# Loading w_in and the first v's through SyncE's queue in 4 bytes, with the rounding on ScalarE

## The chip, the cores and the metric

The kernel runs on one core of a Trainium2 chip. The metric is the device time of one execution in microseconds (us). The core has TensorE (PE; its weight loads are listed as PEld), VectorE (DVE), ScalarE (ACT), GpSimd (POOL) and SyncE (SP). Transfers are issued by SyncE's queue, by ScalarE's queue or by GpSimd, and are carried by 16 DMA engines.

## The reference

The work has two stages. The first is a gated linear attention over 4 batches, 8 heads, 768 positions and 48 channels, in float32:

```python
f = 1.0 / (1.0 + np.exp(-f_logit))
for t in range(S):
    state = f[:, :, t, :, None] * state + np.einsum('bhd,bhe->bhde', k[:, :, t], v[:, :, t])
    y[:, :, t] = np.einsum('bhd,bhde->bhe', q[:, :, t], state)
```

The second takes y as 3072 rows of 384 and runs a two-layer network with a rational function between the layers:

```python
h = x @ w_in                      # 384 x 2048
P = a[0] + a[1] * h + a[2] * h2 + a[3] * h3
Q = 1.0 + np.abs(b[0]) * np.abs(h) + np.abs(b[1]) * h2
g = P / (Q + 1e-06)
return (g @ w_out).astype(np.float32)   # 2048 x 384
```

## The kernel before, in words

The 3072 positions are cut into 12 units of 256 (two blocks of 128): unit n is part n // 4 of batch n % 4. For a unit the kernel does the following.

- It loads f, k, q (float32, SyncE's queue) and v (rounded to bf16 on the way, GpSimd's queue). Each has three buffers, taken in turn.
- ef and ls (ScalarE) make the logarithm of the gate, cs (TensorE) its sums along the positions, A (ScalarE) the exponentials of the sums, xa (VectorE, and GpSimd for k of later units) the products of q and k with them. T and Te transpose them and copy them out; sc and mk are the scores and their mask; ic, si, ae and st carry the state; vm (GpSimd) copies parts of v; yi and yb (TensorE) make y; ye (ScalarE) scales it to bf16 as x.
- h multiplies x with w_in in four groups of four columns of blocks; hy (ScalarE) copies each group out of PSUM to bf16. The rational function follows: sq, ab, p1, p2, pm, gm and some additions on VectorE; lz, ln and ex (logarithm and exponential in place of the division) on ScalarE; zd and ta, additions that are done by accumulating transfers of GpSimd's queue.
- o multiplies with w_out, oe copies the sums to an output buffer osb, and so stores it by SyncE's queue in two transfers of 64 partitions.

There is no planner at run time. The string ORDER (L19) lists all steps, and L568 runs through it: the order of a step among those of its own engine or queue is the order of execution there, and semaphores hold each step until its inputs are there and its buffer is free. Where steps of different engines stand to each other in the string has no effect of itself. "@n" names the PSUM slot of a step.

The names that matter here:

- load (L197): `ld n what` issues the load of f, k, q or v of unit n. A load of q, k or f of a whole unit is 393 KB; units 0's are issued in halves.
- load_w_in (L207): `wi m0 m1` issues three transfers on GpSimd's queue that read float32 and write bf16, each for one third kk of the rows of w_in and 1024 columns. Their list on the memory's side is `[[96 * d_ff, HP], [d_ff, 32], [1, n]]`, with HP = 4 and n = 1024: 4 times 32 rows of 4,096 bytes. On the chip they fill 128 partitions.
- ye (L430) writes x into one of two buffers, oe (L545) writes into one of two output buffers, store (L551) sends them out.
- lq (float32, the logarithm's output), the ring z of two and the ring g of three (bf16) are buffers of the rational function; each has 16 x 256 elements a partition.

Of the kernel before, what the change touches and what calls it, by code (L numbers as in the profile page):

```python
# [8 lines left out]
F32 = mybir.dt.float32  # L9
BF16 = mybir.dt.bfloat16  # L10
# [14 lines left out]
ld 2 k; cs 2 @3; xa 1 1; xa 1 0; sc 0 0 @2; A 2 1; fb; vm 0 0; T 1 @0; A 2 0; mk 0 0; ae 2; fr; mk 0 1
si 1 0 @3; ic 1; yi 0 1 @2; st 1 0; yb 0 2 4; Te 1; yb 0 0 2; ld 4 f; sc 1 0 @1; ye 0 s; ld 3 v; sc 1 1 @0
mk 1 0; si 1 1; vm 1 1; vm 1 0; h 0 0 4 @2; mk 1 1; ld 2 v; st 1 1; xa 2 0; h 0 4 8 @1; hy 0 0 4; ld 4 q
yi 1 1 @0; hy 0 4 8; yb 1 2 4; yb 1 0 2; ab 0 0 8; ef 3; h 0 12 16 @3; sq 0 0 8; ye 1 s; ld 3 q; ls 3
h 0 8 12 @2; zv 0 0 8; hy 0 12 16; cs 3 @1; xa 2 1; hy 0 8 12; h 1 4 8 @0; lz 0 0 8; ld 6 f; sq 0 8 16
h 1 8 12 @3; p1 0 0 16; ld 5 k; hy 1 4 8; si 2 0 @2; ab 0 8 16; A 3 0; T 2 @0; ld 3 k; pm 0 0 16; hy 1 8 12  # L30
Te 2 s; h 1 12 16 @3; ld 5 f; p2 0 0 16; ic 2; ld 5 q; ae 3; hy 1 12 16; h 1 0 4 @0; zv 0 8 16; ef 4; ta 0 8 16
ld 4 k; A 3 1; sc 2 0 @3; st 2 0; hy 1 0 4; xa 3 0; yi 2 1 @1; mk 2 0; xa 3 1 0 4 p; lz 0 8 16; sc 2 1 @0
si 2 1; mk 2 1; vm 3 1; ls 4; ic 3 @3; vm 2 1; st 2 1; vm 2 0; ex 0 0 16; ld 4 v; yb 2 2 4; sq 1 0 16; si 3 0
ta 0 0 8; yb 2 0 2; cs 4 @0; wo 12 16; ab 1 0 16; T 3 @2; wo 0 4; ae 4; vm 3 0; st 3 0; ye 2 s; wo 8 12
p1 1 0 16; si 3 1; A 4 1; h 2 0 4 @1; wo 4 8; Te 3 s; st 3 1; pm 1 0 16; h 2 4 8 @3; A 4 0; sc 3 0 @2; hy 2 4 8
u 1 12 16 @0; p2 1 0 16; hy 2 0 4; h 2 12 16 @3; ln 1 12 16; xa 4 0; ta 1 8 16; sc 3 1 @1; ef 5; mk 3 0
h 2 8 12 @0; xa 4 1 0 4 p; hy 2 12 16; mk 3 1; ls 5; yi 3 1 @2; yb 3 0 2; hy 2 8 12; gm 0 0 16; yb 3 2 4; ld 8 f
cs 5 @3; ye 3 s; ic 4 @1; ae 5; A 5 1; ab 2 0 16; h 3 8 12 @0; ef 6; A 5 0; zv 1 0 8; u 1 8 12 @2; hy 3 8 12
o 0 0 8 12 @3; sq 2 0 16; ln 1 8 12; si 4 0; h 3 4 8 @0; ls 6; lz 1 0 8; T 4 @2; p1 2 0 16; zd 2 0 8; o 0 1 0 4
st 4 0; xa 5 1 0 4 p; hy 3 4 8; Te 4; si 4 1; o 0 1 8 12; ex 1 0 16; st 4 1; sc 4 0 @0; ta 1 0 8; sc 4 1 @2  # L40
pm 2 0 16; o 0 0 12 16; zd 2 8 16; h 3 0 4 @1; ld 6 v; p2 2 0 16; o 0 0 4 8; ld 5 v; hy 3 0 4; o 0 1 4 8; ef 8
o 0 1 12 16; mk 4 1; ta 2 8 16; h 3 12 16 @1; lz 2 0 8; xa 5 0; o 0 0 0 4; vm 4 0; mk 4 0; vm 4 1; hy 3 12 16
yi 4 1 @2; yi 4 0; gm 1 0 16; yb 4 0 2; oe 0 0 2 s; yb 4 2 4; so 0 0 2; cs 6 @0; ye 4 s; ld 6 q; h 4 4 8 @1
ld 6 k; A 6 0; sq 3 0 16; lz 2 8 16; h 4 0 4 @3; ld 7 f; p1 3 0 16; ae 6; h 4 8 12 @2; hy 4 4 8; hy 4 0 4
ab 3 0 16; si 5 0 @1; ic 5; A 6 1; T 5 @3; tv 2 0 8; hy 4 8 12; zd 3 8 16; o 1 0 12 16 @0; st 5 0; ex 2 0 16
ld 7 q; o 1 0 0 4; pm 3 0 16; o 1 1 4 8; h 4 12 16 @2; ld 8 q; zv 3 0 8; o 1 0 4 8; hy 4 12 16; si 5 1
o 1 1 0 4; p2 3 0 16; o 1 1 12 16; Te 5 s; o 1 1 8 12; gm 2 0 16; ta 3 0 8; lz 3 8 16; ta 3 8 16; sc 5 1 @2
ld 7 k; sc 5 0 @3; o 1 0 8 12; vm 5 0; st 5 1; xa 6 1 0 4 p; ld 9 f; mk 5 1; o 2 0 0 4 @1; lz 3 0 8; o 2 1 12 16
mk 5 0; vm 5 1; ic 6 @2; vm 6 1; ls 8; sq 4 0 16; yi 5 0 @3; yi 5 1; oe 1 0 2 s; o 2 1 8 12; ef 7; o 2 0 4 8
ex 3 0 16; yb 5 0 2; xa 6 0; yb 5 2 4; o 2 1 4 8; ab 4 0 16; ld 8 v; si 6 0; o 2 0 12 16; p1 4 0 16; ld 7 v  # L50
T 6 @0; so 1 0 2; o 2 0 8 12; ld 8 k; ye 5 s; vm 6 0; st 6 0; zd 4 0 8; p2 4 0 16; ls 7; si 6 1; o 2 1 0 4
Te 6 s; h 5 12 16 @3; st 6 1; zv 4 8 16; cs 7 @2; oe 2 0 2 s; pm 4 0 16; h 5 0 4 @0; A 7 0; so 2 0 2; ld 10 f
hy 5 12 16; h 5 8 12 @1; hy 5 0 4; ld 11 f; gm 3 0 16; h 5 4 8 @3; ae 7; hy 5 8 12; A 7 1; sc 6 1 @0; xa 7 0
# [47 lines left out]
def kernel(  # L101
# [12 lines left out]
    nc = tc.nc  # L114
    B, H, S, D = q.shape
# [494 lines left out]
```

## Time and profile before

| | |
|---|---|
| median of 2 runs | 233.36 us (232.94 to 233.78) |
| the profiled execution | 232.19 us |
| its span | 230.5 us |
| granted TensorE clock, mean | 0.999 |
| busy: PE / PEld | 196.3 (85%) / 141.8 (61%) |
| busy: DVE | 204.2 (89%) |
| busy: ACT | 195.8 (85%) |
| busy: POOL | 84.8 (37%) |
| SyncE's queue (q1) | 40,976 packets, 18.88 MB |
| GpSimd's queue (q0) | 22,800 packets, 23.87 MB |
| the six w_in transfers, issue to landing | 13.1 us in the median (11.8 to 18.6) |

Busy time is the time in which an engine has an instruction in work; shares are of the span. The profile lists times from the span's start. The megabytes of the queues are those written: a transfer that rounds from 4 bytes to 2 reads twice as much. Besides the page the trace has a record of each packet (queue, size, start, duration) and of each landing, the semaphore update that tells that a transfer is complete.

By windows of 10 us the busy time is, in us:

| window | PE | DVE | ACT | POOL |
|---|---|---|---|---|
| 0 to 10 | 2.13 | 3.67 | 5.73 | 5.48 |
| 10 to 20 | 7.24 | 4.44 | 3.80 | 3.21 |
| 20 to 30 | 5.00 | 6.35 | 1.90 | 0.00 |
| 30 to 40 | 10.00 | 8.24 | 7.28 | 2.29 |
| 40 to 50 | 7.46 | 10.00 | 10.00 | 3.00 |

### The profile page before, as it was taken

The numbers are of one execution on the slowest core, as the hardware profiler recorded it, in microseconds if no ns is written. First come the engines' busy times: TensorE is split into PE (matmuls) and PEld (weight loads), VectorE is DVE, ScalarE is ACT, GpSimd is POOL, SyncE is SP. The second block draws the span as 40 slices with busy tenths as digits, with TensorE's granted clock in tenths as the row PEclk, the third lists the DMA queues.
The fourth block names the chain that finished last, engine by engine and source line by source line (L and its number), as shares of the span: only waits on it lengthen the run. The fifth ranks groups of instructions, "written<-read, shape, count | busy, mean of one in ns | idle before, by whom it ended". The sixth has DMA issues, their size and how long they took to land.

```text
span 230.5 us, 6995 instructions
## 1 busy us (share of the span) xinstructions
PE 196.3 (85%) x3112; PEld 141.8 (61%) x3112; DVE 204.2 (89%) x184; ACT 195.8 (85%) x183; POOL 84.8 (37%) x102
## 2 busy tenths in 40 slices
PE   0493599867999999899999988999996998899992
PEld 0362378646676777477767747767865675665550
DVE  5251788999999999999999999999999999989860
ACT  4751139999999999999999998999997995999960
POOL 7420030089408701733575394143370332311000
PEclk9999999999999999999999999999999999999999
DMA  6999999999996999999999899999973899998235
GB/s 139 221 218 186 187 201 218 251 193 147 179 215 129 165 176 274 263 231 254 275 221 240 213 165 179 149 240 184 164 149 70 170 179 196 205 204 167 74 81 124
DMA packets 64094, 43.19 MB, mean 187 GB/s; under 512 B 53696, under 2 KB 58816, under 8 KB 64064
## 3 DMA queue, kind: packets, MB, share of 16 engines
q0 software_dynamic: 22800, 23.87, 65.0%
q1 hardware_dynamic: 40976, 18.88, 34.9%
q8 instruction: 24, 0.39, 0.7%
q10 hardware_dynamic: 288, 0.00, 0.1%
q14 instruction: 6, 0.05, 0.1%
HBM read 25.17 MB, written 4.72 MB: 130 GB/s over the span
## 4 chain that ended last, share of the span: by engine, by line
DVE 45%; ACT 19%; DMA 14%; issue 11%; PE 6%; SPq 3%; DVEq 0%; ACTq 0%; POOLq 0%
DVE g L533 7%; DMA q<-in_q_dram 7%; DVE h L471 6%; DVE scm L358 6%; ACT lq L501 6%; DVE g L521 5%; ACT qi L506 4%; DMA z<-h 4%; PE hp L455 4%; DVE g L511 4%; DVE hy L516 4%; ACT hy L467 3%; SPq L204 3%; DVE z L475 3%; DMA g<-hy 3%
## 5 line engine op out<-in xcount | busy, mean ns | idle before, releaser
L455 PE MATMUL hp<-x,w_in_sb 128*128 128x256 bf16 x576 | 68.0, 273 | 4.0 <-ACT x L434 1.7
L542 PE MATMUL op<-w_out_sb,g 128*128 128x384 bf16 x384 | 69.2, 326 | 1.3 <-issue 0.7
L455 PEld LDWEIGHTS <-w_in_sb 128*128 128x128 bf16 x576 | 55.9, 98 | 15.7 <-issue 6.1
L467 ACT CAST hy<-hp 128x1024 bf16<-128x1024 f32 x48 | 49.2, 1073 | 4.1 <-PE hp L455 4.1
L542 PEld LDWEIGHTS <-g 128*128 128x128 bf16 x384 | 36.1, 98 | 25.5 <-issue 2.6
L501 ACT ACTIVATE lq<-z 128x2048 f32<-128x2048 bf16 x22 | 43.0, 1983 | 2.7 <-DMA z<-h 2.7
L506 ACT ACTIVATE qi<-lq 128x4096 bf16<-128x4096 f32 (+1 forms) x14 | 44.5, 3187 | 0.1
L525 POOL DMA_DIRECT2D g<-hy x19 | 18.2, 1105 | 51.3 <-ACT hy L467 21.8
L497 POOL DMA_DIRECT2D z<-h x16 | 15.4, 967 | 41.2 <-DVE z L475 11.8
L521 DVE TENSOR_TENSOR g<-g,h 128x4096 bf16<-128x4096 bf16 (+1 forms) x13 | 29.4, 2259 | 0.0
L358 DVE TENSOR_TENSOR scm<-sc,mask 128x1024 bf16<-128x1024 f32 x24 | 28.3, 1210 | 0.7 <-PE sc L350 0.7
L471 DVE TENSOR_TENSOR h<-hy 128x4096 bf16<-128x4096 bf16 (+1 forms) x13 | 27.5, 2116 | 1.1 <-ACT hy L467 1.1
L533 DVE TENSOR_TENSOR g<-g,qi 128x4096 bf16<-128x4096 bf16 (+1 forms) x14 | 27.7, 1978 | 0.9 <-ACT qi L506 0.8
L310 ACT ACTIVATE A<-cs 128x768 f32<-128x768 f32 (+1 forms) x26 | 20.3, 809 | 9.0 <-DVE qkp L315 9.0
L204 POOL DMA_DIRECT2D v<-in_v_dram x12 | 13.9, 1214 | 20.6 <-PE y L371 17.1
L315 POOL TENSOR_TENSOR qkp<-k,A 128x768 bf16<-128x768 f32 x9 | 18.4, 2049 | 6.6 <-ACT A L310 6.6
L329 PE MATMUL tp<-ident,qkp 128*128 128x128 bf16 x192 | 14.7, 234 | 6.8 <-DVE qkp L315 6.5
L511 DVE TENSOR_SCALAR g<-hy,a_sb 128x4096 bf16<-128x4096 bf16 x12 | 18.1, 1509 | 0.1
L315 DVE TENSOR_TENSOR qkp<-q,A 128x768 bf16<-128x768 f32 (+1 forms) x13 | 11.6, 898 | 6.8 <-ACT A L310 3.8
L329 PEld LDWEIGHTS <-qkp 128*128 128x128 bf16 x192 | 12.4, 105 | 8.5 <-DVE qkp L315 7.0
L516 DVE TENSOR_SCALAR hy<-hy,a_sb 128x4096 bf16<-128x4096 bf16 x12 | 16.8, 1402 | 0.0
L365 POOL COPY vmp<-v 128x128 bf16<-128x128 bf16 x24 | 14.5, 676 | 4.8 <-DMA v<-in_v_dram 3.6
(69 smaller groups left out, 252.6 us busy)
## 6 DMA issues: line engine op xcount, KB each, us to landing
g<-hy POOLq DMA_DIRECT2D x19, 512.0 KB, 7.7
z<-h POOLq DMA_DIRECT2D x16, 512.0 KB, 6.6
f<-in_f_logit_dram SPq DMA_DIRECT2D x11, 384.0 KB, 7.6
k<-in_k_dram SPq DMA_DIRECT2D x11, 384.0 KB, 7.4
q<-in_q_dram SPq DMA_DIRECT2D x11, 384.0 KB, 8.0
out_dram<-osb SPq DMA_DIRECT2D x22, 192.0 KB, 6.4
v<-in_v_dram POOLq DMA_DIRECT2D x12, 192.0 KB, 7.6
w_in_sb<-in_moe_w_in_dram POOLq DMA_DIRECT2D x6, 256.0 KB, 13.1
```

Source lines behind the costliest of these rows:

```text
L315: i = (nc.gpsimd if eng == "p" else nc.vector).tensor_mul(s["qk"][:, x, :, hh, 0:D], s["qk"[x]][:, hh].rearrange("p h i d -> p i h d"), s[ ...
L329: nc.tensor.transpose(t[:, x, i, p, :], s["qk"][:, x, i, 2 * p:2 * p + 2, :].rearrange("t h d -> t (h d)"), ident)
L358: return nc.vector.tensor_mul(t, s["sc", g].rearrange("s r a i t -> s (r a) (i t)"), mb)
L455: nc.tensor.matmul(t[:, m - m0, :].rearrange("f (j t) -> f j t", j=UB), w_in_sb[:, kk, m * P:(m + 1) * P], s["x"][:, :, kk, :], start=(kk ...
L467: nc.scalar.copy(fl(big(s, "hy"), m0, m1), fl(s["hp", m0], 0, m1 - m0))
L471: return nc.vector.tensor_mul(fl(big(s, "h2"), m0, m1), fl(big(s, "hy"), m0, m1), fl(big(s, "hy"), m0, m1))
L501: nc.scalar.activation(fl(lq, m0, m1), fl(big(s, "z"), m0, m1), AF.Ln, scale=regs[2], bias=1.0 + 1e-6)
L506: nc.scalar.activation(fl(qi, m0, m1), fl(lq, m0, m1), AF.Exp, scale=-1.0)
L511: return nc.vector.tensor_scalar(fl(big(s, "g"), m0, m1), fl(big(s, "hy"), m0, m1), a_sb[:, 3:4], a_sb[:, 2:3], op0=ALU.mult, op1=ALU.add)
L521: return nc.vector.tensor_mul(fl(big(s, "g"), m0, m1), fl(big(s, "g"), m0, m1), fl(big(s, "h2"), m0, m1))
L533: return nc.vector.tensor_mul(fl(big(s, "g"), m0, m1), fl(big(s, "g"), m0, m1), fl(qi, m0, m1))
L542: nc.tensor.matmul(s["op", g][:, j, 0:DM], big(s, "g")[:, m, C * j:C * j + C], w_out_sb[:, m, :], start=(s["on", j] == 1), stop=(s["on", j ...
```

## The change

- w_in is loaded by SyncE's queue as float32, in six parts (wl), into buffers that are not yet used for anything else: four parts in lq, two in the third buffer of g. ScalarE rounds each part to bf16 into w_in_sb (wc).
- v of units 0 and 1 is loaded by SyncE's queue as float32 (vl) into the second buffer of z, and rounded by ScalarE into its own buffer (vc). v of the later units stays as it was.
- x has four buffers instead of two. The outputs have one buffer instead of two; units 9 to 11 use the three buffers of f in its place.
- The order on TensorE and on VectorE is the same. GpSimd's loses its six loads. ScalarE's gains the eight casts. SyncE's gains the eight loads, and the stores of unit 5 go ahead of those of unit 6 instead of behind them. PSUM slots are the same four, dealt out a little otherwise.

The steps of the two queues and of ScalarE where they differ, in their order (`+` is new, `-` is gone):

```diff
 SyncE
 ld 0 f 0 2
+vl 0
 ld 0 f 2 4
 ld 0 k 0 2
 ld 1 f
 ld 0 q 2 4
 ld 0 q 0 2
 ld 0 k 2 4
+vl 1
 ld 2 f
 ld 1 k
+wl 0 0 8
+wl 1 0 8
+wl 2 0 8
 ld 1 q
+wl 0 8 16
 ld 2 q
+wl 1 8 16
+wl 2 8 16
 ld 3 f
 ld 2 k
...
+so 5 0 2
 so 6 0 2
-so 5 0 2
 GpSimd
 cu 1
-ld 0 v
 ci
-ld 1 v
 vm 0 1
-wi 0 8
-wi 8 16
 vm 0 0
 ScalarE
 ab_ a a
+vc 0 s
 ef 1
...
 ae 0 2 4
+vc 1 s
 ae 1
...
 ls 2
+wc 0 0 8 s
 A 2 1
+wc 1 0 8 s
 A 2 0
+wc 2 0 8 s
 ae 2
 fr
+wc 0 8 16 s
 ye 0 s
+wc 1 8 16 s
+wc 2 8 16 s
 hy 0 0 4
```

The functions:

```diff
-    rings("x", 2, [UB, KD, C], BF16)
+    rings("x", 4, [UB, KD, C], BF16)
-    rings("osb", 2, [UB, DM], F32)
+    rings("osb", 1, [UB, DM], F32)
...
+    def w_part(kk, m0, m1):
+        i = kk + KD * (m0 // 8)
+        t = lq[:, 4 * i:4 * i + 4, :].rearrange("p m t -> p (m t)") if i < 4 else (
+            ring["g"][2][:, 8 * (i - 4):8 * (i - 4) + 8, :].rearrange("p m t -> p (m t)").bitcast(F32))
+        return t[:, 0:(m1 - m0) * P]
+
+    def load_w_part(kk, m0, m1):
+        return nc.sync.dma_start(out=w_part(kk, m0, m1),
+                                 in_=bass.AP(tensor=moe_w_in.tensor,
+                                             offset=moe_w_in.offset + 32 * kk * d_ff + m0 * P,
+                                             ap=[[96 * d_ff, HP], [d_ff, 32], [1, (m1 - m0) * P]]))
+
+    def cast(eng, dst, src):
+        return {"s": nc.scalar.copy, "v": nc.vector.tensor_copy, "p": nc.gpsimd.tensor_copy}[eng](dst, src)
+
+    def cast_w_part(kk, m0, m1, eng):
+        return cast(eng, w_in_sb[:, kk, m0 * P:m1 * P], w_part(kk, m0, m1))
+
+    def v_part(n):
+        return ring["z"][1][:, 6 * n:6 * n + 6, :].rearrange("p m t -> p (m t)").bitcast(F32)
+
+    def load_v_part(n):
+        s = unit(n)
+        t0 = s["c"] * NT
+        return nc.sync.dma_start(out=v_part(n).rearrange("p (h e) -> p h e", h=H),
+                                 in_=v[s["b"], :, t0:t0 + NT, :].rearrange("h (p i) d -> p h (i d)", i=2))
+
+    def cast_v_part(n, eng):
+        s = unit(n)
+        s["v"] = ring["v"][n % len(ring["v"])]
+        return cast(eng, s["v"].rearrange("p h i d -> p (h i d)"), v_part(n))
...
-        s["osb"] = ring["osb"][n % len(ring["osb"])]
+        s["osb"] = ring["osb"][0] if n < UNITS - 3 else (
+            ring["f"][n % 3].rearrange("p h i d -> p (h i d)").rearrange("p (j d) -> p j d", j=UB))
```

More of the change, by code (lines that the diff above doesn't have):

```diff
@@ L25 @@
[L25 to L29, printed above, removed]
@@ new lines @@
+hy 0 0 4; xa 2 0; yi 1 1 @0; yb 1 2 4; hy 0 4 8; ld 3 q; yb 1 0 2; ef 3; h 0 12 16 @2; ab 0 0 8; ye 1 s
+sq 0 0 8; h 0 8 12 @3; ls 3; zv 0 0 8; hy 0 12 16; ld 6 f; cs 3 @1; hy 0 8 12; xa 2 1; h 1 4 8 @0; lz 0 0 8
+sq 0 8 16; ld 5 k; h 1 8 12 @2; p1 0 0 16; ld 3 k; hy 1 4 8; si 2 0 @3; ab 0 8 16; A 3 0; T 2 @0; ld 5 f
+pm 0 0 16; hy 1 8 12; Te 2 s; h 1 12 16 @2; ld 5 q; p2 0 0 16; ic 2; ae 3; ld 4 k; hy 1 12 16; h 1 0 4 @0
+zv 0 8 16; ef 4; ta 0 8 16; A 3 1; sc 2 0 @2; st 2 0; hy 1 0 4; xa 3 0; yi 2 1 @1; mk 2 0; xa 3 1 0 4 p
@@ new lines @@
+yb 3 2 4; ld 8 f; cs 5 @2; ye 3 s; ic 4 @1; ae 5; A 5 1; ab 2 0 16; h 3 8 12 @0; ef 6; A 5 0; zv 1 0 8
+u 1 8 12 @3; hy 3 8 12; o 0 0 8 12 @2; sq 2 0 16; ln 1 8 12; si 4 0; h 3 4 8 @0; ls 6; lz 1 0 8; T 4 @3
+p1 2 0 16; zd 2 0 8; o 0 1 0 4; st 4 0; xa 5 1 0 4 p; hy 3 4 8; Te 4; si 4 1; o 0 1 8 12; ex 1 0 16; st 4 1
+sc 4 0 @0; ta 1 0 8; sc 4 1 @3; pm 2 0 16; o 0 0 12 16; zd 2 8 16; h 3 0 4 @1; ld 6 v; p2 2 0 16; o 0 0 4 8
+ld 5 v; hy 3 0 4; o 0 1 4 8; ef 8; o 0 1 12 16; mk 4 1; ta 2 8 16; h 3 12 16 @1; lz 2 0 8; xa 5 0; o 0 0 0 4
@@ new lines @@
+vm 4 0; mk 4 0; vm 4 1; hy 3 12 16; yi 4 1 @3; yi 4 0; gm 1 0 16; yb 4 0 2; oe 0 0 2 s; yb 4 2 4; so 0 0 2
+cs 6 @0; ye 4 s; ld 6 q; h 4 4 8 @1; ld 6 k; A 6 0; sq 3 0 16; lz 2 8 16; h 4 0 4 @2; p1 3 0 16; ae 6
+h 4 8 12 @3; hy 4 4 8; hy 4 0 4; ld 7 f; ab 3 0 16; si 5 0 @1; ic 5; A 6 1; T 5 @2; tv 2 0 8; hy 4 8 12
+zd 3 8 16; ld 7 q; o 1 0 12 16 @0; st 5 0; ex 2 0 16; o 1 0 0 4; pm 3 0 16; ld 8 q; o 1 1 4 8; h 4 12 16 @3
+zv 3 0 8; o 1 0 4 8; hy 4 12 16; si 5 1; o 1 1 0 4; p2 3 0 16; o 1 1 12 16; Te 5 s; o 1 1 8 12; gm 2 0 16
@@ new lines @@
+h 5 0 4 @0; gm 3 0 16; oe 2 0 2 s; A 7 0; so 2 0 2; h 5 8 12 @1; hy 5 12 16; xa 7 0; ld 10 f; hy 5 0 4
+h 5 4 8 @3; ld 11 f; ld 9 k; ae 7; hy 5 8 12; sc 6 1 @0; A 7 1; sc 6 0 @1; mk 6 1; hy 5 4 8; cs 8 @2; ld 9 q
+xa 7 1 0 4 p; mk 6 0; lz 4 8 16; o 3 0 12 16 @0; o 3 0 8 12; ta 4 0 8; ab 5 0 16; ld 10 k; T 7 @3; A 8 0
+ta 4 8 16; sq 5 0 16; yi 6 1 @1; ef 9; yi 6 0; o 3 1 8 12; ae 8; A 8 1; o 3 0 4 8; Te 7 s; yb 6 2 4; p1 5 0 16
+yb 6 0 2; ic 7 @2; lz 4 0 8; sc 7 1 @3; ye 6 v; vm 8 0; vm 7 1; si 7 0; o 3 1 4 8; xa 8 1 0 4 p; st 7 0
@@ new lines @@
+hy 9 8 12; p1 8 0 16; lz 7 8 16; zd 8 0 8; h 9 12 16 @0; vm 10 0; st 10 0; vm 10 1; Te 10; vm 11 0
+o 6 0 12 16 @3; hy 9 4 8; zd 8 8 16; o 6 1 4 8; pm 8 0 16; hy 9 12 16; sc 10 0 @1; sc 10 1 @2; ex 7 0 16
+o 6 1 0 4; o 6 1 12 16; mk 10 0; xa 11 1 0 4 p; h 9 0 4 @0; mk 10 1; o 6 0 4 8; hy 9 0 4; p2 8 0 16
+yb 10 2 4 @1; yb 10 0 2; lz 8 0 8; T 11 @2; gm 7 0 16; ta 8 0 8; yi 10 1; yi 10 0; ta 8 8 16; o 6 0 0 4; ye 10 s
+o 6 0 8 12; Te 11 s; sq 9 0 16; o 6 1 8 12; o 7 1 12 16 @0; lz 8 8 16; o 7 0 12 16; ab 9 0 16; h 10 8 12 @1
@@ new lines @@
+p1 9 0 16; oe 6 0 2 s; zd 9 0 8; sc 11 0 @2; hy 10 8 12; o 7 0 4 8; so 6 0 2; vm 11 1; mk 11 0; o 7 0 0 4
+ex 8 0 16; zd 9 8 16; h 10 4 8 @3; pm 9 0 16; h 10 12 16 @1; h 10 0 4 @2; p2 9 0 16; hy 10 12 16; o 7 1 8 12
+hy 10 4 8; gm 8 0 16; ta 9 0 8; si 11 0 @1; hy 10 0 4; ic 11; ta 9 8 16; sc 11 1 @3; o 7 1 4 8; lz 9 0 8
+st 11 0; yi 11 0 @2; mk 11 1; yi 11 1; yb 11 0 2; lz 9 8 16; ab 10 0 16; yb 11 2 4; o 7 1 0 4; sq 10 0 16
+o 7 0 8 12; ye 11 s; o 8 1 0 4 @1; ex 9 0 16; o 8 1 8 12; h 11 0 4 @3; p1 10 0 16; zd 10 0 8; zd 10 8 16
@@ L92 @@
+ex 11 0 8; o 10 0 4 8; o 9 1 4 8; gm 10 8 16; o 10 0 0 4; oe 9 0 2 s; tv 11 0 8; lz 11 8 16; o 10 1 12 16
+so 9 0 2; o 10 0 12 16; gm 11 0 8; o 10 1 8 12; ex 11 8 16; o 10 1 0 4; pm 11 8 16; o 11 1 0 4 @0; o 11 0 0 4 @3
+tv 11 8 16; o 11 1 4 8; o 10 0 8 12; gm 11 8 16; o 11 0 4 8; oe 10 0 2 s; o 11 1 12 16; so 10 0 2; o 11 1 8 12
+o 11 0 12 16; oe 11 1 2 v; o 11 0 8 12; so 11 1 2; oe 11 0 1 s; so 11 0 1
 """
@@ L562, in behind @@
                           reason="begins behind it")
-    steps = dict(ld=load, wi=load_w_in, wo=load_w_out, ab_=load_ab, cu=const_u, ci=const_i, cm=const_m,
+    steps = dict(wl=load_w_part, wc=cast_w_part, vl=load_v_part, vc=cast_v_part, ld=load, wi=load_w_in, wo=load_w_out, ab_=load_ab, cu=const_u, ci=const_i, cm=const_m,
                  cz=const_z, fa=coef_a, fb=coef_b, fr=coef_r, ef=ef, ls=ls, cs=cs, A=A, xa=xa, T=T, Te=Te,
```

106 lines of the change are left out of this document (39 added, 67 removed).

## The prediction, on record before the result

> **What bounds it now.** I read the slices first: which engine is full, and when.
>
> ```profile
> span 230.5 us, 6995 instructions
> ...
> PE   0493599867999999899999988999996998899992
> ...
> DVE  5251788999999999999999999999999999989860
> ACT  4751139999999999999999998999997995999960
> ```
>
> A slice is 5.8 us. From the eighth on (40 us) VectorE and ScalarE stand at 9 nearly to the end, in an order fixed by hand: a microsecond gained or lost before 40 us goes through to the end, since nothing has room to take it up. Before 40 us all engines wait. What for stands in the chain of waits, start and length in us:
>
> ```profile
> 8.83 15.50 DMA q<-in_q_dram
> 24.33 0.02 issue
> 24.35 0.96 DVE qkp L315
> ...
> 31.38 2.94 PE hp L455 x24
> 34.33 1.01 ACT hy L467
> ```
>
> The start is a transfer: q of unit 1 needs 15.5 us from issue. After it come its product, the masks of unit 0, y, x, the first hp, and hy. The timeline has the two rows that I measure the start by, and the earlier wait for k of unit 1:
>
> ```profile
> 4.52 0.52 ACT L282 ACTIVATE f<-f 128x384 f32<-128x384 f32 x1 [2.43 <-DMA f<-in_f_logit_dram]
> ...
> 20.38 0.96 DVE L315 TENSOR_TENSOR qkp<-k,A 128x768 bf16<-128x768 f32 x1 [4.03 <-DMA k<-in_k_dram]
> ...
> 33.02 1.01 ACT L467 CAST hy<-hp 128x1024 bf16<-128x1024 f32 x1 [2.43 <-PE hp L455]
> ```
>
> The first hy at 33.02 is my mark: ScalarE then works without a pause to 39.3, where VectorE takes over full. Why the transfers are slow stands in the DMA view of 12 to 18 us; beneath it the same row of 40 to 46 us, when SyncE's queue (q1) is alone. Columns: packets, MB, share of 16 engines.
>
> ```profile
> q0 software_dynamic: 1118, 0.67, 77.1%
> q1 hardware_dynamic: 1570, 0.59, 44.3%
> ```
>
> ```profile
> q1 hardware_dynamic: 4010, 1.52, 109.1%
> ```
>
> While GpSimd's w_in (q0) runs, SyncE's queue moves 0.59 MB in 6 us; alone it moves 1.52 MB, which is 1.55 us for a load of 393 KB. So w_in holds back k and q of unit 1.
>
> **The change, part by part.**
>
> *v of units 0 and 1, in 4 bytes.* Two SyncE loads of 1.55 us instead of two of GpSimd, ahead of k of unit 1. Two ACT casts of 128x768, about 0.85 us each by the 0.81 of x and 0.87 of lsp (L434, L287). ScalarE is busy 3.8 us from 10 to 20 and 1.9 from 20 to 30, so they lie in its idle time. The second cast waits for v of unit 1 at about 13.0 and holds back the four A and f steps behind it, which end at 15.6, before k lands. On the path: only the bytes, counted below.
>
> *GpSimd loses* two issues of v (1.07 and 0.92 us) and six of w_in (0.66 each). It then idles until 30.3 anyway: nothing.
>
> *k of unit 1.* Ahead of it and with it SyncE's queue has 8 loads' worth. The first half load lands at 4.52, so k lands at 4.52 + 7.5 x 1.55 = 16.1 instead of 20.3.
>
> *w_in by SyncE, in 4 bytes.* Six parts, each of 128 packets of 4,096 bytes: three behind k, one behind q of unit 1, two behind q of unit 2, then the loads of units 3 and on. A packet: the trace's packet records have a median of 172 ns for GpSimd's 768 of w_in, which read the same 4,096 bytes; SyncE's output packets of 1,536 bytes took 62 at least and 75 in the median, which makes 165 to 200 for 4,096. I take 172. Over how many engines? The trace does not show this form on SyncE. The memory side of a part is a list of 4 x 32 rows, the outermost count 4. SyncE's loads have 128 there and its stores 64, and each was spread over 16: of q1's 40,976 packets 36,864 are load rows and 3,072 output rows, and the 1,040 left are 65 transfers (39 loads, 26 stores) x 16 completions. GpSimd spread these very lists over at least 0.771 x 16 = 12.3 engines. So the ends are 16 engines, 128 x 0.172 / 16 = 1.4 us a part (the list's nearest row), and 4, 32 x 0.172 = 5.5 us (if the queue deals out the outermost count). Who makes the packets is the queue, and no SyncE row shows it cutting a count finer than its outermost; I take 4. [...]
>
> *The sum with four engines.* SyncE's loads land in the order of issue (from k of unit 1 on at 20.29, 24.33, 29.01, 31.60), so whatever stands behind a part waits for its share on those four. Landings: k 16.1; three parts 21.6, 27.1, 32.6; q of unit 1 at 34.2; fourth part 39.7; q of unit 2 41.2; the last two 46.7 and 52.2. Then the v of units 3 and 2, issued by GpSimd from about 40 on, share the four engines: 128 packets of 36 ns on each, 4.6 us, at most half of it before the last part; I add 1 of 0 to 2.3.
>
> *The casts of w_in.* ScalarE has them in line: three before ae of unit 2, the fourth before x of unit 0, the last two before the first hy. Each 1.05 us by L467's 1.01 to 1.07 for 128x1024. Behind the sixth waits everything of ScalarE; behind hy waits VectorE's whole body. x of unit 0 is made after the fourth, at 41; the first hp is ready at 43; the first hy starts at 52.2 + 1 + 1.05 = 54.3, 21.3 later than 33.02. f of unit 3 (1.55 behind the sixth part) is needed 2 us after hy begins, k and the next ones later: they are just in time.
>
> *Four buffers of x.* x is overwritten two units later today, long after its hp; no row of L434 waits for that: nothing.
>
> *One buffer of outputs.* The copy of unit 2 (106.64) would wait for the stores of unit 1, which landed at 108.58: 1.9 us of ScalarE, full there. If they land sooner, 0. The others have 10 us and more, or (units 9 to 11) f's buffers.
>
> *Stores of unit 5 ahead of unit 6's.* They go at 163 instead of beside unit 6's at 185, where a z landed after 10.5 us instead of 6.6 (median) and ScalarE waited 2.48 us for it. Gain 0 to 2.5. I set this against the copy of unit 2: zero, and both ends into the range.
>
> Sum: the profiled execution took 232.19 (span 230.5 and 1.7 around it), 1.2 under the median of 233.36. 232.19 + 21.3 = **253.5**. Its own range: packets of 165 and no sharing with v take 2.3 off, the stores 2.5: 248.7; packets of 200 and full sharing add 6.7: 260.2.
>
> **Rivals.**
>
> *Sixteen engines (the other side).* Parts of 1.4 us: q of unit 1 lands at 16.1 + 4.2 + 1.55 = 21.9 and w_in is complete at 27.6. From q to the first hy stand 8.7 us today (24.33 to 33.02): hy at 30.6. On ScalarE x ends at 28.2 and two casts at 30.3, in time. 2.4 us earlier, 229.8. If the packets run at the 1.52 MB in 6 us of small ones, a part takes 2.1 us and hy comes at 32.7: 231.9. With the stores' ends 227.3 to 233.8. It decides on the number of engines: even at a part of 2.1 us, which is 10 to 11 engines at 172 ns. For it: GpSimd's 12.3 on the same lists. Against it: SyncE's counts.
>
> *Sixteen engines, and the one output buffer costs the gain.* ScalarE stalls 1.9 at unit 2 and the stores of unit 5 bring nothing: 229.8 + 1.9 = 231.7, and up to 234 with parts of 2.1 us. No change. For it: the landing at 108.58 behind a full queue.
>
> **Chances.** Four engines 0.66, sixteen 0.20, sixteen with the buffer's stall 0.08; 0.06 for something between or beyond. Slower by over 2% takes the first and most of the rest, 0.71; within 2%, which is 4.7 us and about what a measurement of this kernel can tell from no change, 0.25; faster 0.04. The likeliest case alone ranges over 248.7 to 260.2; both signs hold chance, so the range goes from 229 to 259.
>
> **What would show it.** q1's packets: 36,864 + 2,048 + 768 + 3,072 rows and 73 transfers x 16 completions are 43,920; with six of the transfers on four engines 43,848. The parts' time to landing: over 10 us and growing with four, under 9 with sixteen. k of unit 1 used at 16 to 17 in both. The wait ahead of the first hy: a cast of w_in held by its DMA (four), or nothing on ScalarE (sixteen). From 60 us on the slices should look like today's, shifted. The prediction is wrong if SyncE's queue spreads a list of 4 x 32 rows as it spreads 128, or if the engines make up late work after 60 us.

## The result, and the profile after

| | before | after |
|---|---|---|
| median of 2 runs | 233.36 us (232.94 to 233.78) | 252.92 us (252.61 to 253.22) |
| ratio to before, 95% interval | | 1.084 (1.074 to 1.094) |
| the profiled execution / its span | 232.19 / 230.5 us | 252.61 / 250.9 us |
| first hy begins | 33.02 us | 55.33 us |
| SyncE's queue (q1) | 40,976 packets, 18.88 MB | 43,848 packets, 22.81 MB |
| granted TensorE clock, mean | 0.999 | 0.932 |

The change makes the kernel 8.4% slower. In the tables and comparisons below, runs over 1.5% above the fastest of their kernel are left out of the ratios, so that a ratio can differ a little from the quotient of the medians.

From the page of the kernel after, the slices (6.3 us each) and SyncE's queue (packets, MB, share of 16 engines):

```profile
span 250.9 us, 7002 instructions
...
PE   0291019419869999999989999899989799799992
...
DVE  5170038208999999999999999999999999999970
ACT  2862123139999999999979999999999899699970
PEclk9997555957988999999999999999999999999999
...
q1 hardware_dynamic: 43848, 22.81, 35.9%
```

VectorE and ScalarE are full from the eleventh slice on (63 us) to the end, as they were from the eighth of 5.8 us before. What has grown is the hollow part ahead of it. In it the chain of waits of the kernel after reads (start and length in us):

```profile
13.86 21.34 DMA q<-in_q_dram
...
35.23 0.96 DVE qkp L351
...
37.06 0.69 ACT w_in_sb L234
37.76 19.57 DMA f<-in_f_logit_dram
...
57.34 0.84 ACT f L318
```

Two loads of SyncE's queue, q of unit 1 and f of unit 3, make up 41 us of the start. Neither is large: each has 393 KB, and what makes them late stands in the queue ahead of them. The timeline of ScalarE shows what that is. In square brackets is the idle time before the row and what ended it:

```profile
23.00 1.04 ACT L234 CAST w_in_sb<-lq 128x1024 bf16<-128x1024 f32 x1 [5.58 <-DMA lq<-in_moe_w_in_dram]
...
28.02 1.04 ACT L234 CAST w_in_sb<-lq 128x1024 bf16<-128x1024 f32 x1 [3.27 <-DMA lq<-in_moe_w_in_dram]
...
40.26 1.04 ACT L234 CAST w_in_sb<-lq 128x1024 bf16<-128x1024 f32 x1 [2.22 <-DMA lq<-in_moe_w_in_dram]
41.22 0.80 ACT L470 ACTIVATE x<-y 128x768 bf16<-128x768 f32 x1
48.01 1.04 ACT L234 CAST w_in_sb<-g 128x1024 bf16<-128x1024 f32 x1 [5.99 <-DMA g<-in_moe_w_in_dram]
54.38 1.04 ACT L234 CAST w_in_sb<-g 128x1024 bf16<-128x1024 f32 x1 [5.33 <-DMA g<-in_moe_w_in_dram]
55.33 1.92 ACT L503 CAST hy<-hp 128x1024 bf16<-128x1024 f32 x2
...
130.44 0.80 ACT L585 COPY osb<-op 128x768 f32<-128x768 f32 x1 [1.49 <-DMA out_dram<-osb]
...
216.34 1.91 ACT L537 ACTIVATE lq<-z 128x2048 f32<-128x2048 bf16 x1 [1.95 <-DMA z<-h]
```

The casts of w_in wait for their parts one after the other, and the first hy stands right behind the sixth cast, 22.3 us later than before. The first two casts are 5.02 us apart: that is the time of one part of 512 KB. f of unit 3 at 57.34 stands right behind the first two hy, so the last part and f come in together and the chain could name either.

From there on the kernel after is the kernel before, shifted. At the copy of unit 2's outputs ScalarE has a wait of 1.49 us (last rows but one), and its shift against before is 130.44 − 106.64 = 23.8. At the z of unit 9 it is 216.34 − 195.64 = 20.7, and at the end 250.9 − 230.5 = 20.4. Most of what was gained between comes from one instruction that was long in the profile of before. VectorE's timeline of before, and then of after, at the same step p1:

```profile
135.63 3.08 DVE L511 TENSOR_SCALAR g<-hy,a_sb 128x4096 bf16<-128x4096 bf16 x1
```

```profile
158.60 1.34 DVE L547 TENSOR_SCALAR g<-hy,a_sb 128x4096 bf16<-128x4096 bf16 x1
```

The shift is 22.97 ahead of it and 21.23 at the next step (159.86 − 138.63). In both kernels GpSimd makes its product of k (qkp) beside this p1, before and then after:

```profile
135.82 1.80 POOL L315 TENSOR_TENSOR qkp<-k,A 128x768 bf16<-128x768 f32 x1
```

```profile
159.04 2.58 POOL L351 TENSOR_TENSOR qkp<-k,A 128x768 bf16<-128x768 f32 x1 [2.53 <-ACT ae L478]
```

One of the two is long each time, and this is so in all 14 traces of this document. In the six kernels with two output buffers p1 takes 3.08 to 3.09 us and the product 1.80 (2.32 in v_only). In the eight with one output buffer p1 takes 1.33 to 1.34 us and the product 2.58 to 2.82. This looks as if one waited for the other. What decides which of them waits, and how the output buffer bears on it, is not shown.

### The profile page after: what moved, and what is told of

Read it like the earlier page. It is cut to its first block, busy times and chain, and to the rows that moved or that the text cites. A ratio compares the mean times of both kernels' runs of the same rounds, so it can differ in the third digit from the quotient of the medians.

```text
span 250.9 us, 7002 instructions
## 1 busy us (share of the span) xinstructions
PE 198.2 (79%) x3109; PEld 143.2 (57%) x3112; DVE 202.2 (81%) x184; ACT 203.1 (81%) x191; POOL 76.3 (30%) x94
## 3 DMA queue, kind: packets, MB, share of 16 engines
q1 hardware_dynamic: 43848, 22.81, 35.9%
## 4 chain that ended last, share of the span: by engine, by line
DVE 40%; DMA 20%; PE 14%; ACT 10%; issue 8%; SPq 5%; POOL 0%; ACTq 0%; DVEq 0%
DMA q<-in_q_dram 9%; PE op L578 8%; DMA f<-in_f_logit_dram 8%; DVE h L507 7%; DVE scm L394 5%; DVE g L557 5%; DVE g L547 4%; DVE g L569 4%; DMA z<-h 4%; DVE hy L552 4%; SPq L205 4%; DVE z L511 3%; DVE qkp L351 3%; PE hp L491 3%; ACT hy L503 2%
## 5 line engine op out<-in xcount | busy, mean ns | idle before, releaser
L491 PE MATMUL hp<-x,w_in_sb 128*128 128x256 bf16 x576 | 70.4, 278 | 12.1 <-ACT w_in_sb L234 8.7
L491 PEld LDWEIGHTS <-w_in_sb 128*128 128x128 bf16 x576 | 57.1, 100 | 23.6 <-ACT w_in_sb L234 9.0
L561 POOL DMA_DIRECT2D g<-hy x19 | 17.6, 973 | 59.3 <-ACT hy L503 32.5
L351 DVE TENSOR_TENSOR qkp<-q,A 128x768 bf16<-128x768 f32 (+1 forms) x13 | 11.5, 890 | 22.3 <-DMA q<-in_q_dram 16.6
L511 DVE TENSOR_SCALAR z<-hy 128x4096 uint16<-128x4096 uint16 (+1 forms) x13 | 14.8, 1142 | 12.0 <-ACT hy L503 12.0
L333 PE MATMUL cs<-lsp,Ui 128*128 128x384 bf16 (+1 forms) x39 | 12.1, 373 | 7.7 <-ACT lsp L323 7.2
```

The lines of the kernel that those rows point to most:

```text
L351: i = (nc.gpsimd if eng == "p" else nc.vector).tensor_mul(s["qk"][:, x, :, hh, 0:D], s["qk"[x]][:, hh].rearrange("p h i d -> p i h d"), s[ ...
L491: nc.tensor.matmul(t[:, m - m0, :].rearrange("f (j t) -> f j t", j=UB), w_in_sb[:, kk, m * P:(m + 1) * P], s["x"][:, :, kk, :], start=(kk ...
```

## The experiments

They ask four things: whether the number of engines is what makes a part slow, whether the parts are what sets the start, what the other pieces of the change are worth, and whether the start can be made shorter. Twelve kernels were run. Each was timed beside the kernel before on the same chip; the medians of before were 234.27 us for the first four, 233.37 for q_first, v_only, out_only and hold_k, 234.0 for pool_parts, so5_only and w_between, and 234.17 for w_between2.

### How many engines carry a part

The list of a part on the memory's side is changed alone: 16, 8 or 2 as its outermost count instead of 4. outer16:

```diff
-                                             offset=moe_w_in.offset + 32 * kk * d_ff + m0 * P,
-                                             ap=[[96 * d_ff, HP], [d_ff, 32], [1, (m1 - m0) * P]]))
+                                             offset=moe_w_in.offset + 8 * kk * d_ff + m0 * P,
+                                             ap=[[24 * d_ff, 16], [d_ff, 8], [1, (m1 - m0) * P]]))
```

outer8 has `16 * kk * d_ff` and `[[48 * d_ff, 8], [d_ff, 16], ...]`, outer2 `64 * kk * d_ff` and `[[192 * d_ff, 2], [d_ff, 64], ...]`. These three kernels leave out the right order of the rows of w_in on the partitions, so they compute another product. They price the transfer and cannot take the kernel's place.

> Only the list of a w_in part changes: 16 x 8 rows in place of 4 x 32 (same bytes, same 128 packets of 4,096 bytes, same transfers, casts and order; other rows of w_in come to lie on a partition, so the product is another one and the time is all that counts). Theory, the queue deals a part out by the outermost count: 16 engines, 1.3 us a part in place of 5.1; the six parts land by 29 us, the first hy starts at 32 to 34, and the kernel takes 229 to 232, q1 has 43,920 packets. Rival, 4-byte loads of w_in on SyncE's queue or the casts on ScalarE are what costs: 252 to 253 as with 4 x 32.

> As before with 8 x 16 rows (the product is another one). Theory: 8 engines, 16 packets of 160 ns on each, 2.6 us a part; q of unit 1 lands at 27, the last part at 36, first hy at 37 to 38, kernel 234 to 237, q1 has 43,872 packets. Rival (4 bytes or casts): 252 to 253.

> As before with 2 x 64 rows (the product is another one). Theory: 2 engines, 64 packets of 160 ns on each, 10.2 us a part; last part at 82 to 86, first hy at 84 to 88, kernel 281 to 286, q1 has 43,836 packets. Rival (4 bytes or casts): 252 to 253.

One stretch of 2 to 4 us each, in which almost nothing but parts of w_in moved, in the DMA view of the kernel after (22 to 26 us), of outer2 (20 to 24), outer8 (20 to 22) and outer16 (18 to 20); columns as above:

```profile
q1 hardware_dynamic: 105, 0.42, 25.8%
```

```profile
q1 hardware_dynamic: 51, 0.21, 12.8%
```

```profile
q1 hardware_dynamic: 65, 0.27, 51.1%
```

```profile
q1 hardware_dynamic: 134, 0.49, 101.7%
```

Of 16 engines 25.8% are 4.1, 12.8% are 2.0, 51.1% are 8.2 and 101.7% all of them. The packets of the whole run say the same without any time in it. q1 has 42,752 rows and 67 other transfers of 16 completions each; six parts on 2, 4, 8 or 16 engines add six times as many:

| outermost count | 42,752 + 67 x 16 + 6 x count | q1 packets | median of a w_in packet | first hy | median time | ratio to before (95%) |
|---|---|---|---|---|---|---|
| 2 | 43,836 | 43,836 | 162 ns | 84.17 us | 282.89 us | 1.214 (1.199 to 1.230) |
| 4 (after) | 43,848 | 43,848 | 166 ns | 55.33 us | 252.92 us | 1.084 (1.074 to 1.094) |
| 8 | 43,872 | 43,872 | 276 ns | 45.24 us | 243.44 us | 1.045 (1.031 to 1.058) |
| 16 | 43,920 | 43,920 | 273 ns | 35.40 us | 234.40 us | 1.005 (1.000 to 1.010) |

The packet counts agree to the packet, and the time follows. So in these four runs on SyncE's queue the outermost count of the list sets how many engines carry the transfer, and with 16 in place of 4 nearly the whole loss is gone. The step from 4 to 16 is worth 18 us here, and is still no gain over before.

That last point was expected otherwise. outer16 was to run in 229 to 232 us and outer8 in 234 to 237, because a packet was taken at about 160 ns. With 8 and 16 engines it takes 273 to 276, so a part takes 128 x 273 / 16 = 2.2 us instead of 1.3, and six parts 13.1 us of SyncE's queue. In outer16, ScalarE's timeline shows that they still decide:

```profile
32.21 0.81 ACT L470 ACTIVATE x<-y 128x768 bf16<-128x768 f32 x1 [1.97 <-PE y L407]
32.91 1.04 ACT L234 CAST w_in_sb<-g 128x1024 bf16<-128x1024 f32 x1
34.45 1.04 ACT L234 CAST w_in_sb<-g 128x1024 bf16<-128x1024 f32 x1 [0.49 <-DMA g<-in_moe_w_in_dram]
35.40 1.92 ACT L503 CAST hy<-hp 128x1024 bf16<-128x1024 f32 x2
```

Three things end close together: x of unit 0 (it follows q of unit 1, used at 26.50), the last part (a wait of 0.49) and the casts themselves, two of which stand between x and hy. The first hy comes 2.4 us later than before (33.02).

split32 keeps the original rows on each partition and gets 16 engines in another way, by 12 transfers of 32 partitions each:

```diff
-                                             ap=[[96 * d_ff, HP], [d_ff, 32], [1, (m1 - m0) * P]]))
...
+        for a in range(HP):
+            t = w_part(kk, m0, m1)[32 * a:32 * a + 32]
+            made.append(nc.sync.dma_start(
+                out=bass.AP(tensor=t.tensor, offset=t.offset, ap=[t.ap[0], [n, last - kk], [1, n]]),
...
+                            ap=[[d_ff, 32], [32 * d_ff, last - kk], [1, n]])))
```

> The right rows on the right partitions with the outermost count 32: one transfer for each block of 32 partitions, 12 transfers for w_in in place of 6 (three thirds at once for the first half, one and two for the second). Theory: every transfer uses 16 engines, and this takes as long as 16 x 8 rows plus six issues of 0.5 us that lie under the transfers: 229 to 232. Rival: filling 32 partitions at a time is slower than filling 128, by up to the ratio 4 of partitions: then 240 to 253.

Measured: 237.15 us (235.36 to 238.17, 4 runs), ratio 1.016 (1.004 to 1.027). It has 44,016 packets in q1, which is 42,752 + 79 x 16: the 12 transfers are on 16 engines each. Its packets take 313 ns in the median instead of outer16's 273, which is 768 x 40 / 16 = 1.9 us more for all of w_in, and the first half lands as one piece, so that the first cast comes at 24.66 us and not at 18.99. The first hy is at 39.14. The time lies between what was expected (229 to 232) and the rival (240 to 253). So of the two ways to 16 engines, the one that reaches all 128 partitions in one transfer was the faster by some 3 us. How much of that is the 32 partitions and how much the grouping of the parts was not taken apart.

pool_parts leaves the list of 4 x 32 rows and the 4 bytes and changes the queue alone:

```diff
-        return nc.sync.dma_start(out=w_part(kk, m0, m1),
+        return nc.gpsimd.dma_start(out=w_part(kk, m0, m1),
```

> The changed kernel with the six w_in parts issued by GpSimd in place of SyncE: the same lists of 4 x 32 rows, the same 4 bytes, buffers and casts. Tells the queue from the list. Theory, it is SyncE's queue that deals a part out by the outermost count, and GpSimd's spreads the same list over 16 engines as it does in the kernel before: parts are there by 32 to 35, first hy at 34 to 38, kernel 233 to 239. Rival, the list of 4 x 32 rows in plain 4-byte form has four engines on any queue: first hy at 50 or later, 248 or more.

The DMA view of pool_parts from 20 to 24 us:

```profile
q0 software_dynamic: 245, 0.60, 98.9%
q1 hardware_dynamic: 112, 0.04, 9.6%
```

The same list that occupies four engines on SyncE's queue occupies all of them on GpSimd's (q0), which is 98.9%. So it is the queue with the list, not the list, that sets the number; that part of the expectation held. The time did not: two runs took 245.35 and 249.92 us, which lie too far apart for a ratio, and both are over the 233 to 239 expected. The trace is of the longer one. A packet of w_in took 398 ns in the median there, 2.4 times that of the kernel after, the six parts landed from 29.1 to 50.5 us, and SyncE's k of unit 1, which had to share the engines, was used at 33.42 instead of 17.71. With four times the engines at 2.4 times the packet's time, little is left.

### What sets the start

q_first issues q of unit 1 ahead of the six parts instead of behind three of them:

```diff
 SyncE
 ld 1 k
+ld 1 q
 wl 0 0 8
 wl 1 0 8
 wl 2 0 8
-ld 1 q
 wl 0 8 16
```

> The changed kernel with q of unit 1 issued ahead of the six w_in parts in place of behind the third. Theory, the last w_in part (and the cast behind it, ahead of the first hy on ScalarE) sets the start: q is used at 19 to 20 in place of 35.2, x of unit 0 is still held by the cast of the fourth part, the first hy stays at 53 to 55, the kernel at 251 to 253. Rival, the wait for q of unit 1 (21 us in the chain of waits) is what costs: first hy near 38, kernel near 236.

Measured: 254.02 us (253.16 to 254.87, 2 runs), ratio 1.086 (1.074 to 1.099): no different from after. VectorE's timeline and then the chain of waits of q_first:

```profile
18.75 0.95 DVE L351 TENSOR_TENSOR qkp<-q,A 128x768 bf16<-128x768 f32 x1
```

```profile
35.78 18.34 DMA g<-in_moe_w_in_dram
...
54.14 1.04 ACT w_in_sb L234
55.18 1.83 ACT hy L503 x2
```

q of unit 1 is used at 18.75 us instead of 35.23, and the first hy begins at 55.18 instead of 55.33. The wait for q, which heads the chain of after, was hidden behind w_in; the last part and its cast set the start. The time is 1 us over the 251 to 253 expected.

v_only makes the change of v alone on the kernel before (w_in stays with GpSimd):

```diff
 SyncE
 ld 0 f 0 2
+vl 0
...
 ld 0 k 2 4
+vl 1
 ld 2 f
 GpSimd
-ld 0 v
-ld 1 v
 ScalarE
+vc 0 s
+vc 1 s
```

> The kernel before with only v of units 0 and 1 by SyncE in 4 bytes and rounded on ScalarE; w_in stays with GpSimd. Theory: v costs two loads of 1.5 us on SyncE's queue ahead of k of unit 1 and saves GpSimd's two; k and q of unit 1 still stand beside w_in, which begins no earlier than the two vm copies of unit 0: within 1.5 us of before, 232 to 235. Rival: the slowdown comes from v (its cast stands ahead of the f and A steps on ScalarE): 236 or more.

Measured: 237.07 us (234.86 to 240.04, 10 runs), ratio 1.009 (1.005 to 1.014), above the 232 to 235 expected. VectorE's timeline of v_only:

```profile
23.07 0.96 DVE L333 TENSOR_TENSOR qkp<-k,A 128x768 bf16<-128x768 f32 x1 [5.20 <-DMA k<-in_k_dram]
27.99 0.96 DVE L333 TENSOR_TENSOR qkp<-q,A 128x768 bf16<-128x768 f32 x1 [3.96 <-DMA q<-in_q_dram]
```

k of unit 1 comes 2.7 us and q 3.6 us later than before (20.38 and 24.35): two more loads stand ahead of them in SyncE's queue, at a time when GpSimd's w_in slows that queue (to 0.59 MB in 6 us in the kernel before). The time is that of the rival, 236 or more, but the two rows wait for transfers and not for the casts. In the kernel after GpSimd moves nothing then, and k of unit 1 landed at 16.25 us. So v costs about 1% beside GpSimd's w_in (1.6% by the medians); what it costs in the change itself was not measured by itself.

### The output buffer and the early stores

out_only puts four buffers of x, the one output buffer and the early stores of unit 5 on the kernel before; so5_only moves the stores alone:

```diff
-    rings("x", 2, [UB, KD, C], BF16)
-    rings("osb", 2, [UB, DM], F32)
+    rings("x", 4, [UB, KD, C], BF16)
+    rings("osb", 1, [UB, DM], F32)
...
 SyncE
+so 5 0 2
 so 6 0 2
-so 5 0 2
```

> The kernel before with only the third part of the change: four buffers of x, one of outputs (f's three for units 9 to 11), and the stores of unit 5 ahead of unit 6's. w_in and v are loaded as before. Theory: the copy of unit 2 waits 1.6 to 1.9 us for the stores of unit 1, and the stores of unit 5 no longer lie beside z of unit 9, which gives 1.5 to 2 back: the same as before within 1 us. Rivals: only the stall counts (+1.5 to +2), or only the stores count (-1.5 to -2).

> The kernel before with one step moved: the stores of unit 5 ahead of unit 6's, as in the change (two buffers of outputs, two of x). Theory: the z of unit 9 lands 2 us or more sooner, the wait of 2.48 us ahead of its logarithm goes, 1 to 2.5 us faster than before. Rival: those stores only fill an idle stretch elsewhere, no difference.

so5_only: 232.23 us (230.63 to 233.15, 10 runs), ratio 0.998 (0.992 to 1.003). The stores of unit 5 bring nothing that can be told from no change; a gain of 1 us, the low end of what was expected, lies inside the interval, 2.5 us does not. ScalarE's timeline of so5_only has the logarithm of unit 9:

```profile
196.12 1.91 ACT L501 ACTIVATE lq<-z 128x2048 f32<-128x2048 bf16 x1 [1.73 <-DMA z<-h]
```

The wait ahead of it did not go, it fell from 2.48 to 1.73 us.

out_only: five runs from 229.88 to 237.85 us, too wide a spread for a verdict. The median is 233.58 us; the ratio of 0.985 (0.974 to 0.996) rests on the two shortest runs. The execution with the profile was the longest of the five. ScalarE's timeline of it has the copy of unit 2:

```profile
114.75 0.80 ACT L549 COPY osb<-op 128x768 f32<-128x768 f32 x1 [6.30 <-DMA out_dram<-osb]
```

The same copy waited 1.49 us in the kernel after and not at all in the kernel before, with two buffers. Expected were 1.6 to 1.9. The price of the single buffer is no constant, then; that it goes by how far behind the queues are when unit 1's stores are issued is likely, but not shown. What the four other executions waited is not recorded, so a mean price stays open.

### Can the start be made shorter

The kernel before already has what is needed to order transfers of different queues: a step that ends in `!k` gives its transfer the name k, and a step that ends in `^k` begins when the transfer k has landed. hold_k lets GpSimd's w_in begin when k of unit 1 has landed:

```diff
 SyncE
-ld 1 k
+ld 1 k !k
 GpSimd
-wi 0 8
+wi 0 8 ^k
```

> The kernel before with one thing added: GpSimd begins its w_in transfers once k of unit 1 has landed. Tests whether the start of the kernel before was really held by w_in beside k and q of unit 1, and is meant to be faster than both. Theory: k lands near 15, q of unit 1 near 17 in place of 24.3, w_in's packets begin at 19 to 20 (4.4 us from issue to the first packet before), its first half is there at 25 to 27, the first hy starts at 27 to 30 in place of 33.0: 227 to 230. Rival, what is gained for q is lost because w_in lands later: first hy at 33 or later, no gain.

Measured: 232.87 us (231.09 to 236.43, 10 runs), ratio 0.996 (0.991 to 1.001). k of unit 1 was used at 16.55 us instead of 20.38, q at 17.42 instead of 24.35, x of unit 0 was ready for its scaling at 22.32, and the first hy still began at 31.64, above the 27 to 30 expected. TensorE's and then ScalarE's timeline of hold_k:

```profile
29.29 4.02 PE L455 MATMUL hp<-x,w_in_sb 128*128 128x256 bf16 x18 [2.06 <-DMA w_in_sb<-in_moe_w_in_dram]
```

```profile
31.64 1.01 ACT L467 CAST hy<-hp 128x1024 bf16<-128x1024 f32 x1 [8.51 <-PE hp L455]
```

x waits for w_in now. The first half of w_in landed at 29.24 us; f and k of the next units, which SyncE's queue had behind q, were under way beside it. From there to the first hy it took 2.35 us, 1.0 more than in the next kernel, since the granted clock was 0.50 from 24 to 32 us: 18 matmuls of hp took 4.02 us here, and 22 take 2.58 there. What was held back mostly took the place of what had been late before. The first hy lies between the expectation and its rival (33 or later), and the time is the rival's: no gain.

w_between therefore orders both sides. w_in begins earlier, when k of unit 0 has landed, and f of unit 3 waits until the first half of w_in has. It has the early stores of unit 5 as well, which were worth nothing measurable by themselves.

```diff
 SyncE
-ld 0 k 2 4
+ld 0 k 2 4 !k
...
-ld 3 f
+ld 3 f ^w
 GpSimd
-wi 0 8
+wi 0 8 ^k !w
```

> Meant to beat both kernels: w_in stays with GpSimd (rounded on the way, 16 engines) and begins once the second half of k of unit 0 has landed (12 us; packets from 16 to 17), f of unit 3 and all behind it on SyncE's queue wait until the first half of w_in has landed, and the stores of unit 5 go ahead of unit 6's. Theory: q of unit 1 lands by 18, x of unit 0 is ready at 23, the first half of w_in at 23 to 24, first hy at 25 to 28 in place of 33.0, the stores give 1 to 2: 224 to 228. Rival, the loads of unit 3 become late for ef and xa, and the gain at the first hy is lost again before 60 us: 229 to 233.

Measured: 229.84 us (227.58 to 231.39, 6 runs), ratio 0.982 (0.976 to 0.988): faster than both kernels, by 1.8% than before. That is over the 224 to 228 expected and inside the rival's 229 to 233. ScalarE's timeline of w_between, and then TensorE's:

```profile
26.42 1.01 ACT L467 CAST hy<-hp 128x1024 bf16<-128x1024 f32 x1 [2.29 <-PE hp L455]
...
32.89 0.84 ACT L282 ACTIVATE f<-f 128x768 f32<-128x768 f32 x1 [4.15 <-DMA f<-in_f_logit_dram]
```

```profile
25.11 2.58 PE L455 MATMUL hp<-x,w_in_sb 128*128 128x256 bf16 x22 [0.55 <-DMA w_in_sb<-in_moe_w_in_dram]
```

The first hy begins 6.6 us earlier than before, and the span ends 3.2 us earlier (227.3): f of unit 3, which now waits for w_in, is 4.15 us late for ScalarE, as the rival had it, which would account for the rest. w_between2 holds back the load behind it instead (k of unit 2):

```diff
 SyncE
-ld 3 f ^w
+ld 3 f
-ld 2 k
+ld 2 k ^w
```

> As the kernel in which SyncE's queue waits for the first half of w_in (w_between), but the wait stands one load later: f of unit 3 goes right behind q of unit 2, k of unit 2 and all behind it wait. In w_between the first hy came at 26.4, but f of unit 3 landed only at 32.9 and x of unit 1, which stands behind its exponential on ScalarE, came at 33.6. Theory, that late f gave back 4 of the 6.6 us: f lands by 27, first hy at 27 to 28, x of unit 1 by 31, 3 us or so less than w_between: 225 to 228. Rival, k of unit 2 (needed 4 us later) then lands late instead and takes it back: 228 to 231 as w_between.

Measured: 229.94 us (227.95 to 233.81, 6 runs), ratio 0.983 (0.977 to 0.988), the same as w_between. ScalarE's timeline and then TensorE's of w_between2:

```profile
27.96 1.01 ACT L467 CAST hy<-hp 128x1024 bf16<-128x1024 f32 x1 [4.59 <-PE hp L455]
...
30.67 0.85 ACT L282 ACTIVATE f<-f 128x768 f32<-128x768 f32 x1
```

```profile
25.61 4.11 PE L455 MATMUL hp<-x,w_in_sb 128*128 128x256 bf16 x22 [1.42 <-DMA w_in_sb<-in_moe_w_in_dram]
```

f has no wait any more, and instead the first hy is 1.5 us later. The first half of w_in, which has f of unit 3 beside it now, landed 0.5 us later (25.57 against 25.07). The other 1.0 is TensorE's: the same 22 matmuls took 4.11 us instead of 2.58, at a granted clock of 0.50 from 26 to 28 us, where w_between has 1.00. The second half of w_in landed at 32.08 instead of 30.18. In these traces the bytes that are needed before 32 us set the start, and the clock adds to it; the order can be chosen, and each order tried leaves one of the loads late.

## Why the prediction was right

The forecast was 253.5 us, its own range 248.7 to 260.2; measured were 252.92, and 252.61 for the execution with the profile. The wide range of 229 to 259 had room for the rivals too, so that it tests little; the steps do:

- **Four engines.** Right, and by the reason given, the outermost count: the forecast of 43,848 packets was met exactly, and the series 2, 4, 8, 16 shows it.
- **172 ns a packet.** 166 in the median, 159 with a part alone: such a part took 5.02 us where 5.5 were forecast.
- **Landings.** k of unit 1 landed at 16.25 (16.1 forecast) and was used at 17.71, when VectorE came to it. The first three parts landed at 22.98, 28.00 and 33.88 (21.6, 27.1, 32.6), q at 35.20 (34.2), the fourth part at 40.24 (39.7). Only the second and the fourth part ran nearly alone, in 5.02 and 5.04 us. Beside other loads a packet of a part took 209 to 219 ns in the median (18 to 22 and 30 to 33.9 us), so the first part landed 6.7 us behind k and the third took 5.9.
- **v of units 3 and 2, "1 of 0 to 2.3".** The last part landed at 54.35 instead of 53.2 (52.2 and the 1). The last two parts took 12.75 us together, from the landing of q of unit 2 at 41.60; 12.0 were forecast (two of 5.5 and the 1), and two parts alone would take 10.1. So what shared the engines cost 2.7 us, not 1. While GpSimd's v ran the parts' packets took 172 to 209 ns in the median; other loads of SyncE's queue were under way too, so that all of it is v's is not shown.
- **The casts, 1.05 us each, and hy behind the sixth.** They took 1.04; the last cast and hy overlap by 0.1 us. The first hy came at 55.33, so +22.3 instead of +21.3.
- **x of unit 0 at 41, not on the path.** 41.22, and the first hp was complete at 45.2, 10 us ahead of the first hy. q_first shows that q was hidden: 16 us earlier it moved the first hy by 0.15.
- **f of unit 3 "just in time".** It landed at 57.32 and was used at 57.34, right behind the first two hy.
- **The body carries the shift.** Right in size, +20.4 at the end against +22.3 at the first hy. The step that sets the stores of unit 5 against the one output buffer, zero, does not describe what happened: unit 2's copy lost 1.5, and the wait at the z of unit 9 fell by 0.5 (2.48 to 1.95). Another 1.7 came from the long p1 of before, for which the sum has no term, and 1.2 of the 1.9 that the shift shrinks by are not accounted for by these three. With the microsecond at the first hy they nearly cancel; that the total is within 1 us is in part luck. A gain at the first hy carried less well than this loss: hold_k's 1.4 us left 0.1 at the end, w_between's 6.6 left 3.2, w_between2's 5.1 left 4.2.
- **Four buffers of x.** Nothing in either trace waits for one; not tried alone.
- **The rival of sixteen engines, 229.8 to 231.9.** Its mechanism exists once the list is written for it, but its price was wrong: 234.4. The prediction put the break-even at a part of 2.1 us, which it took to be 10 to 11 engines at 172 ns. The part takes 2.2 us on all sixteen, since a packet takes 273 ns there. Against the kernel before (234.27 on that chip) this is no difference.

## What to carry to other kernels

Write the outermost count of a transfer on SyncE's queue as 16, 32, 64 or 128, which all had 16 completions a transfer here, and read from the queue's packet count how many completions a transfer had: in these runs that gave the number of engines exactly and without any timing. A plain load of 4 bytes with the rounding on an idle engine is no gift even then: it puts the bytes into the queue that also carries the next inputs, and here even sixteen engines brought the time only back to that of the kernel before. Where the start of a kernel is bound by transfers, try the order across the queues. Holding w_in back alone gave nothing (hold_k); holding it back less, and the loads behind it until its first half had landed, gave 1.8%.

## What was not expected of the hardware

- A packet of 4,096 bytes that SyncE's queue reads into the core took 162 and 166 ns with 2 and 4 engines at work, 276 and 273 with 8 and 16. Sixteen engines thus moved 16 x 4,096 / 273 ns = 240 GB/s, not four times the 103 to 105 of four. Since 8 are as slow as 16, it is not simply a limit on the total (8 engines move 133 GB/s in the stretch shown). With 4 engines, packets took 209 to 219 ns beside other loads, too. The cause stays open.
- Packets that read the same 4,096 bytes took 398 ns as plain 4-byte copies by GpSimd's queue, and 172 in the kernel before, where GpSimd rounds them to 2 bytes on the way and writes half as much. That the copy without rounding is the slower one was not expected, and is not explained by these runs. SyncE's loads were under way beside both.
- The granted TensorE clock of the kernel after falls to about half while TensorE waits: 0.53 at 22 to 26 us and 0.50 from 26 to 42, with no matmul from 22 to 34. The page of pool_parts, where TensorE also has no work from 22 to 34 us, seems to show no such fall:

```profile
PE   0273013967779999998889999999989799799992
...
PEclk9999999999999999999999999999999999999999
```

Its matmuls show one. TensorE's timeline of pool_parts has the same transposes at the start and later:

```profile
34.44 1.04 PE L365 MATMUL tp<-ident,qkp 128*128 128x128 bf16 x8 [12.84 <-DVE qkp L351]
...
60.11 1.05 PE L365 MATMUL tp<-ident,qkp 128*128 128x128 bf16 x16 [0.74 <-ACT hy L503]
```

Eight took as long as sixteen did later, so TensorE ran at half its later rate; in the kernel after eight also took 1.04 us, at 36.24 us and a recorded clock of 0.50. The clock records of the trace of pool_parts begin at 45.9 us, and the page shows 9 where it has none. The records of the kernel before begin at 31.9 us, and there too eight took 1.03 us at 25.37; its mean of 0.999 in the table says nothing of its start.

In the kernel after the record falls to 0.50 at 22.25 us, 2.25 us after the end of TensorE's last work at 20.00, in a wait of 16.24 us, and goes back to 1.00 at 42.73. In w_between2 the record falls to 0.50 at 25.4 us, where the wait ahead of hp is only 1.42 us and TensorE was busy for 1.61 of the 2 us from 22 to 24; a wait as long as that of the kernel after is not needed there. What makes the clock fall, and after how long, these runs do not show. The price in the kernel after was small: the first hp was complete 10 us ahead of its copy. In hold_k and w_between2 it stood on the path, with 1.0 us each.
